# The opening of a convolution and feed-forward kernel: x of units 0 and 1 loaded at once, w_in in two column halves, new orders for the first four tiles

## The chip, the core and the metric

The kernel runs on one core of a Trainium2 chip. Such a core has five engines with an instruction queue each: TensorE (PE), VectorE (DVE), ScalarE (ACT), GpSimd (POOL) and SyncE (SP). Here SP issues most of the transfers, POOL issues those of `w_in`, and 16 DMA engines carry all of them. An engine works its queue strictly in order; between engines only semaphores hold things back. Matmuls write to PSUM, from which DVE and ACT read; POOL works on SBUF alone. The metric is the device time of one execution in microseconds (us); lower is better.

## The reference, cut to what matters

```python
batch, seq, d_model = (8, 4096, 192); kernel_size = 7; n_heads = 8        # x, weight
n_tokens, d_model, d_ff = (32768, 192, 2048)                              # w_in, w_out
w = softmax(weight, axis=-1)                                              # 8 heads x 7 taps
x_pad = np.concatenate([np.zeros((B, 6, D)), x], axis=1)
out = np.einsum('hk,bskhg->bshg', w, x_unf)                               # causal convolution along the sequence
h = out.reshape(B * S, D) @ w_in
g = h * np.cos(h)
return g @ w_out
```

All inputs and the output are fp32; the kernel multiplies in bf16.

## The kernel before

The 32,768 tokens are cut into 32 units of 1,024 tokens, and each unit into two tiles of 512, so there are 64 tiles. A unit goes through these stages:

- **Load** (`load_unit`, L72, and `load_edges`, L68): SP transfers x of a unit, 768 KB, and 96 KB of edge rows (16 tokens at each border between blocks of 128). Two buffers.
- **Cast** (`cast_unit`, L175): POOL turns x into bf16 (`x_bf`, two buffers). Half of unit 0 is cast by ACT, at the start.
- **Convolution** (`conv_part`, L214): matmuls with a banded matrix, in two parts of four heads. A part is two PE steps, `c1` and `c2`; then ACT copies each of its two banks to `ct` (L205; `ec1`, `ec2`). In the first two tiles a part is four matmuls over all 128 rows, in one PE step, and a unit has both its parts in one tile, called `d` and `c`.
- **Doubling and turning**: POOL writes a second copy beside each block (`double_unit`, L245), and an SP transposing transfer (`turn_unit`, L249) makes `cT`, the transposed convolution result. POOL then mends the first columns of each block from the edge rows (`mend_edges`, L257).

A tile `t` then runs eight column pairs `j` through three engines:

- PE step `h<j>` (`mm1`, L339): six matmuls, `w_in` columns against `cT`, into a PSUM buffer `h` of two banks. Three such buffers form a ring, which the convolution of later tiles uses too.
- ACT and DVE step `s<j>` (`gcu`, L351): ACT computes the cosine as a shifted sine (L354), DVE multiplies it with `h` (L358) and writes `g`. The buffer `h` is free when DVE is through.
- PE steps `m<n>` (`mm2_step`, L364): n steps of the second product, `g` against `w_out`, into the banks `o_ps0` and `o_ps1`. A phase is 32 steps and fills one half tile; from the second phase on a step is two matmuls on the two row halves of the array, the second belonging to the phase before. In the first phase it is one. At the end of a phase (`q`, `p` in the orders) ACT copies the bank to SBUF (L389; `Q`, `P`), and SP stores every tile.

The order on PE, ACT and DVE is written out by hand as strings. `PE_ORDER` and `ACT_ORDER` hold for all tiles; `PE_FIRST` and `ACT_FIRST` replace them in the first two (called slots t=0 and t=1 here). DVE follows the order of the `s` steps. A word `h0a` is the half `h0` of the first two blocks. The matmul steps are counted through: whatever the order, the 64 tiles hold the same steps, and a later tile starts with 8 steps of its predecessor's phase done.

Before the tiles the kernel builds the band matrix from the softmax of the weights, convolves the first half of unit 0 (`conv_first`, L286) and turns it on PE (`turn_first`, L305). The word `r` in slot 0 stands for `conv_rest` (L318), the other half of unit 0, followed by its doubling and turning, the load of unit 2, and POOL's cast of `w_out` to bf16 (L445).

SP issues in order: x of unit 0, first half (L87); then, behind a wait for DVE's `summed` (L271), its second half and unit 1; then, behind a wait for a copy of `conv_first` (L301), `w_out` in four transfers (L91); the turning of unit 0's second half; units 2 and 3. POOL issues `w_in` early, in two row halves, all columns at once (L84, L134). It casts unit 0's second half at L281 and unit 1 at L332.

Of the kernel before, what the change touches and what calls it, by code (L numbers as in the profile page):

```python
# [11 lines left out]
ALU = mybir.AluOpType  # L12
# [4 lines left out]
def kernel(  # L17
# [8 lines left out]
    nc = tc.nc  # L26
# [7 lines left out]
    NB = T // 128  # L34
    U = 1024
    NU = NTOK // U
    UB = U // 128
# [3 lines left out]
    NP = NF // 2  # L41
# [26 lines left out]
    def load_edges(u, queue=nc.sync):  # L68
        queue.dma_start(out=x_tiles[u][:, UB, :],
                          in_=xf[u * U - 8 : u * U - 8 + U, :].rearrange("(n t) d -> n t d", t=128)[:, 0:16, :])  # L70

    def load_unit(u, n0=0, n1=UB, queue=nc.sync):  # L72
        if n0 == 0:
            x_tiles[u] = xin.tile([128, UB + 1, D], FP32, name="x_f")
        queue.dma_start(out=x_tiles[u][:, n0:n1, :],
                          in_=xf[u * U + n0 * 128 : u * U + n1 * 128, :].rearrange("(n p) d -> p n d", p=128))
# [3 lines left out]
    w = consts.tile([128, NC, NP, 128], BF16)  # L80
    w_src = moe_w_in.rearrange("(m k) (t f) -> t m k f", k=NC, t=2)
    HP = NP // 2

    def load_w(t):  # L84
        nc.gpsimd.dma_start(out=w[64 * t : 64 * t + 64].rearrange("p k j f -> p k (j f)"), in_=w_src[t])

    load_unit(0, 0, NB)  # L87
    wo_f = consts.tile([128, NP, 2, D], FP32)
    wo_src = moe_w_out.rearrange("(i j p) d -> p j i d", i=2, p=128)

# [40 lines left out]
    nc.vector.memset(band, 0.0)  # L131
    for q, copy in enumerate((nc.vector.tensor_copy, nc.scalar.copy, nc.scalar.copy)):
        copy(out=mask[32 * q + 32 : 32 * q + 64], in_=mask[0:32])
    for t in range(2):  # L134
        load_w(t)
    nc.gpsimd.memset(xb0[:, 0, :], 0.0)
    ident = consts.tile([128, 128], BF16)
    nc.gpsimd.memset(ident, 0.0)
# [18 lines left out]
    sync_dep = mybir.DependencyInfo(mybir.DependencyClass.Sync, mybir.DependencyReason.DATA)  # L157
# [17 lines left out]
    def cast_unit(u, n0=0, n1=UB + 1, copy=nc.gpsimd.tensor_copy):  # L175
        bf[u] = xb0 if u == 0 else xbf_pool.tile([128, UB + 1, D], BF16, name="x_bf")

        o = 1 if u == 0 else 0
        copy(out=bf[u][:, n0 + o : n1 + o, :].rearrange("p n (h k r) -> p (n h) k r", k=NC, r=R),  # L179
             in_=x_tiles[u][:, n0:n1, :].rearrange("p n (h r k) -> p (n h) k r", k=NC, r=R))  # L180
        if u and u % UPS == 0:
            nc.gpsimd.memset(bf[u][0:8, UB, :], 0.0)
        bf.pop(u - 2, None)
# [65 lines left out]
    def turn_unit(u, n0=0, n1=UB + 1):  # L249
        ct = ct_tiles.pop(u)  # L250
        if u not in cT:
            cT[u] = cT_pool.tile([128, UB + 1, NC, 128], BF16, name="cT")
        nc.sync.dma_start_transpose(out=cT[u][:, n0:n1].rearrange("p n c k -> p (n c) k"),
                                    in_=ct[:, n0:n1].rearrange("p n c t k -> p (n c t k)"))
        cT.pop(u - 2, None)
# [9 lines left out]
    prod = consts.tile([128, HQ, E, K], BF16)  # L265
    nc.vector.tensor_tensor(out=prod, in0=mask.rearrange("p (o e) k -> p o e k", o=1).to_broadcast([128, HQ, E, K]),
                            in1=wn.rearrange("p h (o k) -> p h o k", o=1).to_broadcast([128, HQ, E, K]), op=ALU.mult)
    diag = consts.tile([128, HQ, E], FP32)
    summed = nc.vector.tensor_reduce(out=diag, in_=prod, axis=mybir.AxisListType.X, op=ALU.add)

    tc.add_manual_dep(nc.sync.nop().ins, summed.ins.name, sync_dep, reason="order of the transfers")  # L271
    load_unit(0, NB, UB)
    load_unit(1)
    load_edges(1)

    three = {"D": nc.vector.tensor_copy, "A": nc.scalar.copy, "P": nc.gpsimd.tensor_copy}
    for i, k in enumerate("DPDPDPADPDPADPAD"):
        q, rows = divmod(i, 4)
        three[k](out=band[32 * rows : 32 * rows + 32, HQ * q : HQ * (q + 1), 32 * rows : 32 * rows + E],  # L279
                     in_=diag[32 * q : 32 * q + 32])  # L280
    cast_unit(0, NB, UB)  # L281
    ct_tiles[0] = ct_pool.tile([128, UB + 1, NC, 2, 64], BF16, name="ct")
    cT[0] = cT_pool.tile([128, UB + 1, NC, 128], BF16, name="cT")
    copies = [nc.scalar.copy, nc.vector.tensor_copy]

    def conv_first():  # L286

        banks = o_banks()
        for half in range(2):
            for h in range(H):  # L290
                for prev in range(2):
                    nc.tensor.matmul(  # L292
                        out=banks[half][:, 0 : 2 * D].rearrange("p (n k h r) -> p h n k r", n=2, k=NC, h=H)[:, h],
                        lhsT=band[:, h, 128 * prev : 128 * prev + 128],
                        rhs=bf[0][:, 2 * half + 1 - prev : 2 * half + 3 - prev, h * G : (h + 1) * G].rearrange(
                            "p n (k r) -> p n k r", k=NC),
                        start=(h == 0 and prev == 0), stop=(h == H - 1 and prev == 1), skip_group_check=True)
            m = copies[half](out=ct_tiles[0][:, 2 * half : 2 * half + 2].rearrange("p n k t w -> p (n k) t w"),  # L298
                             in_=banks[half][:, 0 : 2 * D].rearrange("p (m t w) -> p m t w", t=1, w=64).to_broadcast(
                                 [128, 2 * NC, 2, 64]))  # L300
        tc.add_manual_dep(nc.sync.nop().ins, m.ins.name, sync_dep, reason="order of the transfers")  # L301
        load_wo(0)
        load_wo(1)
# [25 lines left out]
    conv_first()  # L329
    turn_first(0)  # L330
    turn_first(1)
    cast_unit(1)  # L332

# [55 lines left out]
    def store(t, b0=0, b1=2):  # L391
# [8 lines left out]
    PE_ORDER = "h0 m7 c1 m6 c2 m4 h1 m7 q h2 h3 m12 h4 m10 h5 m10 h6 h7 p m8"  # L400
    ACT_ORDER = "s0 ec1 ec2 s1 Q s2 s3 s4 s5 P s6 s7"

    PE_FIRST = ["h0a h0b h1 r h2 h3 h4 d1 d2 h5 h6 c1 c2 h7 p m12",
                "h0 m8 h1 m12 q h2 h3 h4 m4 d1 d2 m8 h5 m8 h6 c1 c2 m8 h7 m4 p m8"]
    ACT_FIRST = ["s0a s0b s1 s2 s3 s4 ed1 ed2 s5 s6 ec1 ec2 s7", "s0 s1 s2 s3 s4 ed1 ed2 s5 s6 ec1 ec2 P s7"]

    HALVES = {"": (0, NB), "a": (0, NB // 2), "b": (NB // 2, NB)}
    step = 0
    for t in range(NT + 2):
        u, second = divmod(t, TPU)  # L410
        cu, cc = (u + TPU, second) if t >= TPU else (1 + t, 1)
        conv = {"c": conv_part(cu, cc, ring_banks if t else o_banks, t < TPU) if cu < NU else iter(())}
        if t < TPU:
            conv["d"] = conv_part(cu, 0, ring_banks if t else o_banks, True)
        act, done, h = (ACT_ORDER if t > 1 else ACT_FIRST[t]).split(), set(), {}

        def flush():
            while act:
                k = act[0]
                need = {"P": "p", "Q": "q", "e": k[1:2] + "2"}.get(k[0], "h" + k[1:])  # L420
                if need not in done:
                    return
                act.pop(0)
                if k == "P" and 0 <= t - 1 < NT:
                    evac(t - 1, 0)
                elif k == "Q" and 0 <= t - 2 < NT:
                    evac(t - 2, 1)
                elif k[0] == "e":
                    next(conv[k[1]], None)
                elif k[0] == "s" and t < NT:  # L430
                    gcu(t, int(k[1]), h.pop(k[1:]), *HALVES[k[2:]])

        for k in (PE_ORDER if t > 1 else PE_FIRST[t]).split():
            if k[0] == "h" and t < NT:
                h[k[1:]] = mm1(t, int(k[1]), *HALVES[k[2:]])
            elif k[0] in conv:
                next(conv[k[0]], None)
            elif k == "r":
                conv_rest()
                double_unit(0, NB, UB)  # L440
                turn_unit(0, NB, UB)
                load_unit(2)
                load_edges(2)
                for q in range(2):
                    nc.gpsimd.tensor_copy(out=wo[:, q * HP : (q + 1) * HP], in_=wo_f[:, q * HP : (q + 1) * HP])  # L445
            elif k[0] == "m":
                for q in range(step, step + int(k[1:])):
                    mm2_step(q)
                step += int(k[1:])
            elif k[0] == "p":  # L450
                assert step % (2 * STEPS) == 0
            elif k[0] == "q":
                assert step % (2 * STEPS) == STEPS
            done.add(k)
            flush()

            if k == "q":
                if second == 0 and t and u + 1 < NU:
                    turn_unit(u + 1)
                    mend_edges(u + 1)  # L460
                if t == 1:
                    turn_unit(1)
                    cast_unit(3)
                    mend_edges(1)
                if second == 0 and u + 3 < NU:
                    cast_unit(u + 3)
                if second == 1 and t > 1 and cu < NU:
                    double_unit(cu)
                if t == NT + 1:
                    store(NT - 1, 1, 2)  # L470
            if k == "p":
                if t < NT + 1 and 0 <= t - 2:
                    store(t - 2)
                if t == NT:
                    store(NT - 1, 0, 1)
                if second == 1 and u + 4 < NU:
                    load_unit(u + 4)
                    load_edges(u + 4)
        if t == 0:
            double_unit(1)  # L480
            load_unit(3)
            load_edges(3)
            cast_unit(2)
        if t == 1:
            double_unit(2)
# [30 lines left out]
```

## Time and profile before

| what | us |
|---|---|
| median of 8 runs (lowest to highest) | 720.67 (720.34 to 720.84) |
| the profiled execution, by its own time | 720.64 |
| its span, first to last instruction | 718.9 |
| PE busy over the span | 707.2 (98%) |
| ACT busy, DVE busy, POOL busy | 617.7, 611.5, 149.7 |
| slot 0 starts on PE / slot 1 / slot 2 / slot 3 / slot 4 | 10.43 / 22.25 / 35.74 / 46.58 / 57.42 |

The profile page gives each engine's busy time, the chain of work that ended last and the costliest groups of instructions. The timeline lists merged instructions in order: start, duration, engine, source line, operation, output and inputs, count, and in brackets the idle time before it with what ended that. A view of windows gives the busy time of each engine in chosen stretches, the granted PE clock, the share of the 16 DMA engines that was busy, and GB/s. All times count from the start of the span. A slot's start in the table is the first matmul of its `h0`. From slot 2 on the slots are 10.84 us apart.

### The profile page before, as it was taken

Reading aid. Unit: us, or ns where it says so; the run is one execution under the profiler, and the core shown is the slowest. Engines: PE = TensorE matmul, PEld = TensorE weight load, DVE = VectorE, ACT = ScalarE, POOL = GpSimd, SP = SyncE. Lnnn points to the kernel's source line nnn. Section 1 sums busy time; section 2 is a strip of 40 time slices with the busy share of each in tenths; the row PEclk is TensorE's granted clock in tenths of the full one; section 3 lists DMA queues with packets and bytes.
Section 4 is the critical chain, followed back from the end, with each engine's and each line's share of the span. In section 5 each row is a group of like instructions: output and inputs, shape, how many; then the busy total and the mean of one; then the engine's idle time right before and its main releaser. Section 6 shows DMA issues by size and latency. Waiting matters only on the chain.

```text
span 718.9 us, 26316 instructions
## 1 busy us (share of the span) xinstructions
PE 707.2 (98%) x11827; PEld 530.1 (74%) x11827; DVE 611.5 (85%) x536; ACT 617.7 (86%) x781; POOL 149.7 (21%) x124
## 2 busy tenths in 40 slices
PE   7899999999999999999999999999999999999997
PEld 3577777777777777777777777777777777777776
DVE  6788888888888888888888888888888888888984
ACT  7888888888898898888888888888888888888884
POOL 5621122221122221122220222220122221121000
PEclk9999999999999999999999999999999999999999
DMA  8755544455534356534455434566434455324312
GB/s 215 182 123 144 133 94 129 86 139 145 123 108 114 92 144 145 111 108 111 105 145 145 116 103 100 117 144 145 108 110 95 124 145 142 103 68 89 80 46 67
DMA packets 183664, 85.24 MB, mean 119 GB/s; under 512 B 111616, under 2 KB 183168, under 8 KB 183552
## 3 DMA queue, kind: packets, MB, share of 16 engines
q1 hardware_dynamic: 183128, 82.78, 46.9%
q8 instruction: 92, 1.51, 0.9%
q0 software_dynamic: 416, 0.79, 0.8%
q14 instruction: 20, 0.16, 0.1%
q10 hardware_dynamic: 8, 0.00, 0.0%
HBM read 31.36 MB, written 25.17 MB: 79 GB/s over the span
## 4 chain that ended last, share of the span: by engine, by line
PE 95%; DMA 2%; POOL 1%; DVE 1%; ACT 0%; issue 0%; SPq 0%; DVEq 0%; POOLq 0%
PE o_ps L377 46%; PE h L347 45%; PE h L190 3%; DMA wo_f<-in_moe_w_out_dram 1%; DMA x_f<-in_x_dram 1%; PE h L377 0%; POOL x_bf L179 0%; DVE band L279 0%; POOL wo L445 0%; DVE g L358 0%; DVEq L511 0%; ACT cs L354 0%; POOL mask L128 0%; DVE ct L298 0%; ACT o_sb L389 0%
## 5 line engine op out<-in xcount | busy, mean ns | idle before, releaser
L358 DVE TENSOR_TENSOR g<-h,cs 128x1024 bf16<-128x1024 f32 (+1 forms) x513 | 603.6, 1218 | 94.1 <-ACT cs L354 89.2
L354 ACT ACTIVATE cs<-h 128x1024 bf16<-128x1024 f32 (+1 forms) x513 | 511.3, 1026 | 59.3 <-PE h L347 52.2
L377 PEld LDWEIGHTS <-g 64*128 64x128 bf16 x8192 | 362.2, 94 | 86.0 <-SPq L164 1.2
L377 PE MATMUL o_ps<-wo,g 64*128 64x192 bf16 x8128 | 423.8, 243 | 1.7 <-ACT o_sb L389 0.6
L347 PE MATMUL h<-cT,w 64*128 64x512 bf16 (+1 forms) x3078 | 398.4, 376 | 0.3 <-DVE cT L316 0.2
L347 PEld LDWEIGHTS <-w 64*128 64x128 bf16 x3078 | 154.7, 94 | 85.4 <-issue 1.1
L259 POOL COPY cT<-cT 128x144 bf16<-128x144 bf16 x31 | 9.5, 307 | 496.0 <-DMA cT<-ct 359.4
L179 POOL CAST x_bf<-x_f 128x1728 bf16<-128x1728 f32 (+1 forms) x32 | 80.5, 2516 | 9.1 <-DMA x_f<-in_x_dram 8.9
L205 ACT CAST ct<-h 128x432 bf16<-128x432 f32 x120 | 56.4, 522 | 27.5 <-PE h L190 26.9
L389 ACT COPY o_sb<-o_ps 128x384 f32<-128x384 f32 x127 | 60.1, 473 | 4.9 <-PE o_ps L377 4.9
L247 POOL COPY ct<-ct 128x1728 bf16<-128x1728 bf16 (+1 forms) x32 | 51.2, 1602 | 18.8 <-ACT ct L205 18.2
L190 PE MATMUL h<-x_bf,band 64*128 64x216 bf16 (+1 forms) x472 | 42.7, 254 | 1.0 <-POOL x_bf L179 1.0
L190 PEld LDWEIGHTS <-band 64*128 64x128 bf16 (+1 forms) x496 | 22.2, 94 | 7.3 <-issue 4.7
L377 PE MATMUL h<-wo,g 64*128 64x192 bf16 x64 | 5.8, 243 | 0.0
L105 PE MATMUL o_ps<-zero 128*128 128x512 bf16 x12 | 4.3, 510 | 1.3 <-DVE zero L100 1.3
L190 PE MATMUL o_ps<-x_bf,band 128*128 128x96 bf16 (+1 forms) x24 | 1.9, 222 | 2.6 <-POOL x_bf L179 2.6
L105 PEld LDWEIGHTS <-zero 128*128 128x128 bf16 x15 | 1.5, 115 | 2.9 <-DVE zero L100 1.3
L205 ACT CAST ct<-o_ps 128x432 bf16<-128x432 f32 (+1 forms) x6 | 2.4, 461 | 1.2 <-PE o_ps L190 1.2
L445 POOL CAST wo<-wo_f 128x1536 bf16<-128x1536 f32 x2 | 2.9, 1470 | 0.8 <-DMA wo_f<-in_moe_w_out_dram 0.8
L292 PE MATMUL o_ps<-x_bf,band 128*128 128x48 bf16 x32 | 1.5, 183 | 1.2 <-ACT x_bf L179 0.8
L292 PEld LDWEIGHTS <-band 128*128 128x128 bf16 x32 | 1.2, 96 | 1.9 <-POOL band L279 1.9
L389 ACT COPY o_sb<-h 128x384 f32<-128x384 f32 x1 | 0.5, 478 | 2.4 <-PE h L377 2.4
(47 smaller groups left out, 27.7 us busy)
## 6 DMA issues: line engine op xcount, KB each, us to landing
out_dram<-o_sb SPq DMA_DIRECT2D x63, 384.0 KB
x_f<-in_x_dram SPq DMA_DIRECT2D x31, 768.0 KB
x_f<-in_x_dram SPq DMA_DIRECT2D x31, 96.0 KB
wo_f<-in_moe_w_out_dram SPq DMA_DIRECT2D x4, 384.0 KB
x_f<-in_x_dram SPq DMA_DIRECT2D x2, 384.0 KB
w<-in_moe_w_in_dram POOLq DMA_DIRECT2D x2, 384.0 KB, 6.3
cT<-ct SPq DMA_TRANSPOSE x32
out_dram<-o_sb SPq DMA_DIRECT2D x2, 192.0 KB
```

Source lines behind the costliest of these rows:

```text
L105: nc.tensor.matmul(out=bank, lhsT=zero[:, 0:128], rhs=zero, start=True, stop=True)
L179: copy(out=bf[u][:, n0 + o : n1 + o, :].rearrange("p n (h k r) -> p (n h) k r", k=NC, r=R), in_=x_tiles[u][:, n0:n1, :].rearrange("p n (h ...
L190: return nc.tensor.matmul(out=ps[i // 2][:, 0 : (n1 - n0) * 2 * G].rearrange("p (n k i r) -> p i n k r", n=n1 - n0, k=NC, i=2)[:, i % 2], ...
L205: copy(o[:, :, 0, :], i[:, :, 0, :])
L247: nc.gpsimd.tensor_copy(out=ct[:, n0:n1, :, 1, :], in_=ct[:, n0:n1, :, 0, :])
L259: nc.gpsimd.tensor_copy(out=cT[u][:, 0:UB, :, 0 : K - 1], in_=cT[u][:, UB].rearrange("p c (n t) -> p n c t", t=16)[:, :, :, 8 : 8 + K - 1])
L347: nc.tensor.matmul(out=h[:, i, n0 * 128 : n1 * 128], lhsT=w[rows, k, j, :], rhs=c[rows, m0 + n0 : m0 + n1, k, :], start=(k == 0), stop=(k ...
L354: nc.scalar.activation(out=cs[:, :, part], in_=h[:, :, part], func=AF.Sin, bias=math.pi / 2.0, scale=1.0)
L358: nc.vector.tensor_tensor(out=g_tiles[t][:, 2 * j : 2 * j + 2, part], in0=h[:, :, part], in1=cs[:, :, part], op=ALU.mult)
L377: m = nc.tensor.matmul(out=o_ps[tt, b][:, si * D : (si + 1) * D], lhsT=g_tiles[tt][rows, f, s * 128 : (s + 1) * 128], rhs=wo[rows, f // 2, ...
L389: nc.scalar.copy(o_sb[t][:, 2 * b : 2 * b + 2, :].rearrange("p s d -> p (s d)"), o_ps.pop((t, b))[:, 0 : 2 * D])
L445: nc.gpsimd.tensor_copy(out=wo[:, q * HP : (q + 1) * HP], in_=wo_f[:, q * HP : (q + 1) * HP])
```

## The change

- SP issues x of unit 0 whole and unit 1 with its edges at the very start, without the wait for `summed`.
- `w_in` is loaded in two column halves, each in two row-half transfers. The first half (columns of `h0` to `h3`) is issued where all of it was; the second (`h4` to `h7`) on POOL behind the cast of unit 0's second half. The cast of unit 1 follows it on POOL, ahead of the work of the tiles.
- In the block `r`, the load of unit 2 is issued on SP ahead of the turning of unit 0's second half instead of behind it.
- `PE_FIRST` and `ACT_FIRST` now cover four slots. Slot 0 holds no second-product steps; `r` comes between `h0a` and `h0b`; the two convolution parts of unit 1 come after `h2` and `h5`. Slot 1 begins with 14 second-product steps. The slots 2 and 3 begin with second-product steps and their convolution, before `h0`. At the start of slot 4 the count of steps is as before.

```diff
-    def load_w(t):
-        nc.gpsimd.dma_start(out=w[64 * t : 64 * t + 64].rearrange("p k j f -> p k (j f)"), in_=w_src[t])
+    def load_w(j0, j1):
+        for t in range(2):
+            nc.gpsimd.dma_start(out=w[64 * t : 64 * t + 64, :, j0:j1, :].rearrange("p k j f -> p k (j f)"),
+                                in_=w_src[t, :, :, j0 * 128 : j1 * 128])
 
     load_unit(0, 0, NB)
+    load_unit(0, NB, UB)
+    load_unit(1)
+    load_edges(1)
...
-    for t in range(2):
-        load_w(t)
+    load_w(0, HP)
...
-    summed = nc.vector.tensor_reduce(out=diag, in_=prod, axis=mybir.AxisListType.X, op=ALU.add)
-
-    tc.add_manual_dep(nc.sync.nop().ins, summed.ins.name, sync_dep, reason="order of the transfers")
-    load_unit(0, NB, UB)
-    load_unit(1)
-    load_edges(1)
+    nc.vector.tensor_reduce(out=diag, in_=prod, axis=mybir.AxisListType.X, op=ALU.add)
...
     cast_unit(0, NB, UB)
+    load_w(HP, NP)
+    cast_unit(1)
...
     turn_first(1)
-    cast_unit(1)
...
-    PE_FIRST = ["h0a h0b h1 r h2 h3 h4 d1 d2 h5 h6 c1 c2 h7 p m12",
-                "h0 m8 h1 m12 q h2 h3 h4 m4 d1 d2 m8 h5 m8 h6 c1 c2 m8 h7 m4 p m8"]
-    ACT_FIRST = ["s0a s0b s1 s2 s3 s4 ed1 ed2 s5 s6 ec1 ec2 s7", "s0 s1 s2 s3 s4 ed1 ed2 s5 s6 ec1 ec2 P s7"]
+    PE_FIRST = ["h0a r h0b h1 h2 d1 d2 h3 h4 h5 c1 c2 h6 h7 p",
+                "m14 h0 m4 h1 m8 h2 m6 q h3 m6 h4 m10 d1 d2 m7 h5 m8 c1 c2 m1 p h6 m2 h7",
+                "m10 c1 m6 c2 m1 h0 m13 q h1 h2 m10 h3 m7 h4 m5 h5 m10 p h6 h7",
+                "m7 c1 m5 c2 m5 h0 m8 h1 m7 q h2 h3 m15 h4 m4 h5 m13 h6 h7 p m8"]
+    ACT_FIRST = ["s0a s0b s1 s2 s3 ed1 s4 ed2 s5 ec1 ec2 s6 s7", "s0 s1 s2 s3 s4 ed1 ed2 s5 ec1 P s6 ec2 s7",
+                 "ec1 ec2 s0 Q s1 s2 s3 s4 s5 P s6 s7", "ec1 ec2 s0 s1 Q s2 s3 s4 s5 P s6 s7"]
...
                 conv_rest()
                 double_unit(0, NB, UB)
-                turn_unit(0, NB, UB)
                 load_unit(2)
                 load_edges(2)
+                turn_unit(0, NB, UB)
```

More of the change, by code (lines that the diff above doesn't have):

```diff
@@ L414 @@
             conv["d"] = conv_part(cu, 0, ring_banks if t else o_banks, True)
-        act, done, h = (ACT_ORDER if t > 1 else ACT_FIRST[t]).split(), set(), {}
+        act, done, h = (ACT_ORDER if t >= len(ACT_FIRST) else ACT_FIRST[t]).split(), set(), {}
         def flush():
@@ L431, in flush @@
                     gcu(t, int(k[1]), h.pop(k[1:]), *HALVES[k[2:]])
-        for k in (PE_ORDER if t > 1 else PE_FIRST[t]).split():
+        for k in (PE_ORDER if t >= len(PE_FIRST) else PE_FIRST[t]).split():
             if k[0] == "h" and t < NT:
```

## The prediction

> **What bounds the kernel now.** I read the page first (its chain of work), then the timeline of the first 60 us, then windows cut at the slots' starts, then windows for the transfers.
>
> ```profile
> PE 95%; DMA 2%; POOL 1%; DVE 1%; ACT 0%; issue 0%; SPq 0%; DVEq 0%; POOLq 0%
> ```
>
> The chain is PE's for 95%, so the run ends when PE has worked off a fixed list of matmuls. An edit to the opening pays by the time at which PE enters slot 4, from where both kernels hold the same work. The windows of slots 0 to 2 (length, busy PE, PEld, DVE, ACT, POOL; granted clock, DMA share, GB/s):
>
> ```profile
> 10.43:22.25 11.82, 8.68 (x89) 4.83 (x91) 9.20 (x11) 9.81 (x16) 7.66 (x6) 1.00 0.98 263
> 22.25:35.74 13.49, 11.78 (x160) 8.10 (x159) 9.72 (x9) 10.30 (x14) 8.13 (x5) 1.00 0.76 191
> 35.74:46.58 10.84, 10.84 (x191) 8.40 (x187) 8.43 (x8) 8.93 (x13) 0.18 (x1) 1.00 0.79 190
> ```
>
> Slot 2 has no idle PE; slots 0 and 1 have 3.14 and 1.71 us of it, while the DMA engines are full in slot 0 (share 0.98). The timeline says who is late:
>
> ```profile
> 2.96 1.40 POOL L85 DMA_DIRECT2D w<-in_moe_w_in_dram  x2
> 11.86 1.22 POOL L179 CAST x_bf<-x_f 128x768 bf16<-128x768 f32 x1 [4.03 <-DMA x_f<-in_x_dram]
> 13.13 0.84 PE L190 MATMUL o_ps<-x_bf,band 128*128 128x96 bf16 x16 [0.97 <-POOL x_bf L179]
> 15.05 2.52 POOL L179 CAST x_bf<-x_f 128x1728 bf16<-128x1728 f32 x1 [1.97 <-DMA x_f<-in_x_dram]
> 17.62 0.53 PE L190 MATMUL o_ps<-x_bf,band 128*128 128x216 bf16 x4 [1.60 <-POOL x_bf L179]
> 18.36 1.57 SPq L253 DMA_TRANSPOSE cT<-ct  x1
> 22.25 0.39 PE L347 MATMUL h<-cT,w 64*128 64x512 bf16 x1
> 29.02 0.53 PE L190 MATMUL h<-x_bf,band 128*128 128x216 bf16 x4 [1.02 <-POOL x_bf L179]
> 35.09 0.84 PE L377 MATMUL o_ps<-wo,g 64*128 64x192 bf16 x16 [0.59 <-ACT o_sb L389]
> ```
>
> Three times a load of x is late, so its cast, so the convolution on PE, and all behind it in PE's queue. The transfers by windows (same columns):
>
> ```profile
> 3.60:4.40 0.80, 0.80 (x3) 0.30 (x2) 0.33 (x3) 0.76 (x3) 0.80 (x3) 1.00 0.06 17
> 4.40:9.40 5.00, 3.73 (x45) 1.98 (x44) 3.88 (x12) 3.88 (x7) 2.36 (x9) 1.00 1.03 145
> 10.20:18.40 8.20, 5.45 (x61) 3.14 (x62) 6.27 (x10) 6.20 (x10) 4.57 (x4) 1.00 1.10 322
> 19.60:21.60 2.00, 1.43 (x13) 0.65 (x12) 1.60 (x2) 2.00 (x5) 1.24 (x2) 1.00 1.04 198
> ```
>
> Full from 4.4 to 18.4: w_in first (to about 10.2, 5.8 us), then x and w_out at 322 GB/s; from 19.6 the turning of unit 0 (2.0 us). Slot 1's `h0` starts at 22.25, 0.65 after the turning's last bytes.
>
> **Unit prices**, from slots 2 and 3: an `h` step 0.65 us of PE (41.67 to 42.32), a second-product step 0.083 (10 in 42.32 to 43.15), a convolution part 0.36 to 0.38; PE start of `h` to ACT 0.87, ACT to DVE 1.05, one multiply to the next 1.14, DVE start to a free ring buffer 1.3.
>
> **Removed: the waits for x.** Unit 0's second half no longer waits for `summed` (over at 5.98), nor its bytes for w_in. x is 1.28 MB behind the first half's last byte at 3.6: 4.0 us at 322 GB/s, 7.6 alone, 10.5 if it shares with the first half of w_in (2.9 us, half of 5.8). POOL is free of its band copies at 7.8; cast 1.2 to 9.05, w_in issue 1.40 to 10.45, unit 1's cast 2.5 to 13.0, against 17.57 before. PE: `h0a` is held by the turned blocks (10.3) and w_in, whose first half lands by about 11.0 (10.5 plus a landing of some 0.5) against 10.68 (a weight load of `h0a` waited for it until then): at most 0.5 later, which slot 1's wait below hides. Then `r` at about 11.5 (13.13 before), unit 1's first part after `h2` at 13.9 with x_bf ready: the waits of 0.97 and 1.60 are gone.
>
> Next is DVE: `s1` at 14.5, then 1.14 each, and 0.9 for ACT's `ec1 ec2` ahead of `s6`: `s7` 21.9 (22.68 before), `h7` on PE 19.2 to 19.85, slot 1's `m14` (14 x 0.083) to 21.0.
>
> **Added: a wait for the turning.** Slot 1's `h0` needs unit 0's second half turned, and that transfer now stands in SP's queue behind unit 2 (0.885 MB), which is behind w_out (1.57 MB); w_in's second half, issued at 9.05, starts 1.44 later (2.96 to 4.4 before), 10.5, and shares the engines. From 10.5: w_in 2.9 + w_out 4.9 + unit 2 2.75 + turning 2.0 = 23.05, and 0.65 to its use: 23.7. On SP it is issued after w_out (13.3 in the timeline) and unit 2's two issues (0.92 + 0.66 there), 14.9; the doubling it needs is done on POOL near 13.8. Both hide under the queue of bytes. POOL's two casts of w_out (1.47 each) follow by about 20, ahead of the second-product steps that need them. One of the 16 engines ran behind before (POOL's cast of w_out at 20.51 waited for it, although the DMA share was 0.18 from 18.4 to 19.6); it could add up to 1.0. I take 24.0. Lower end 22.0: x, w_out and unit 2 at the 367 GB/s of the best stretch near 10.5 to 11.5, w_in's half 2.4, turning 1.8, use 0.5. Upper end 25.0: the lagging engine and halves of w_in at 3.2. So PE idles from 21.0 to 24.0 with all of slot 1 queued behind `h0`, its second-product steps too; ACT and DVE run dry after `s7` (21.9 + 1.2 = 23.1). The gain of slot 0 is spent there.
>
> **Slots 1 to 3 from that `h0` on.** After: 24 `h` 15.6 + 186 steps (14 to 200) 15.4 + convolution 1.5 = 32.5, and stalls that I find by walking the new orders with the prices above: `m2` behind `P`'s copy 0.5, `h7` for a ring buffer 0.2, 0.2 in slots 2 and 3: 33.4. Before: 15.6 + 188 steps 15.6 + 1.5 = 32.7, but 57.42 - 22.25 = 35.17, so 2.5 of stalls (1.02 and 0.59 in the rows above, the rest for ring buffers). The early load of unit 2 (landed by 22, cast by 25, wanted at 30) and the new orders take 1.6 away, two steps done ahead 0.2. The turning of unit 1, issued at `q` (27.5), needs 6 to 8 (25.63 to the mend at 33.62; 61.42 to 67.48): 35.5 at most, used at 36.7.
>
> **Sum.** Slot 4 at 24.0 + 33.4 = 57.4 against 57.42: removed 1.8, added 24.0 - 22.25 = 1.75, net 0.0. The profiled execution took 720.64, 0.03 under the median; I give 720.6. With 22.0 to 25.0: -2.0 to +1.0, its own range 718.6 to 721.6. About 0.2%, 1.44 us, is what a measurement of this kernel tells from no change.
>
> **A rule against the change.** Longest wait in the rows above: 1.60, clock 1.00 in every window; the new wait is near 3. The Trainium skill ("TensorE: Matmul & The Clock Gate", Part 1, what's actually happening) says that after an idle window of about 3.4 us the PE clock halves until it has been busy as long. No row here has such a gap. By the page the sum would be up to 1.7 us more (an estimate, half of 3.4), 722.3; by the rows 720.6.
>
> **Rivals.**
> - *The turning isn't late*: the queue moves it ahead or w_in's halves hide beside x. Then `h0` follows `m14` at 21.0 to 22.0: slot 4 at 54.4 to 55.4, 717.6 to 718.6. For: 367 GB/s was reached. Against: a full share with nothing left to hide in.
> - *w_in's second half is late* (the slower side). `h4` to `h7` and all behind wait for it; wanted at 15.8. Each microsecond past 18.7 moves slot 4 by one, since `m14` ends 5.3 after `h4`: 18.7 + 5.3 = 24.0. If it comes after w_out (10.5 + 4.9 + 2.9 + 0.5 = 18.8): +0.1. If after unit 2 as well (21.5): +2.8, 723.4. For: it's the later issue beside a full SP queue. Against: before, it was x, issued from 6.0 on, that stood back until w_in was through, near 9.4 to 10.2. The Trainium skill ("DMA: Bandwidth & Descriptors", Queues, rings and completion order) has the engines take turns between queues; that row does not show turns, and with turns this half would land near 16.8, costing nothing.
> - *Halved rows of w_in cost per row, not per byte*: 5.8 a half, so the turning is used 2 x 2.9 later, or 2.9 where it hides: +2.9, 723.5. For: 145 GB/s at the start. Against: 276 GB/s from 9.4 to 10.2.
>
> **How the numbers follow.** Turning lands 22.6 to 25.4 (no change beyond 0.2%): 0.45. Not late: 0.25. w_in late 0.12, w_in per row 0.10, the turning past 25.4 for another reason 0.08: 0.30 slower. The range takes the turning at 21.8 below (718.4) and most of the two slower rivals above, to 723.0.
>
> **What would show it.** Right: PE idle some 3 us before slot 1's first `h`, released by DMA cT; unit 1's cast over by 13 to 14; no wait for POOL ahead of the convolutions of slots 0 and 1; slot 4 near 57.4, and 10.84 a slot from there. Wrong: `h0` of slot 1 within 0.5 of `m14`; a wait for DMA w ahead of `h4`; a granted clock under 1.00; or stalls in slots 1 to 3 that my walk does not have.

## The result and the profile after

The median went from 720.53 us (32 executions, 720.20 to 720.99) to **723.13 us** (11 executions, 721.63 to 727.13): a ratio of 1.0037, 95% interval 1.0029 to 1.0046. The kernel became slower by 2.6 us, 0.13 above the upper end of the forecast range. It also became uneven: its executions spread over 5.5 us where those of before spread over 0.8. The profiled execution took 724.66 by its own time (span 722.9), which is 4.02 above the profiled one of before and 1.5 above the median of after.

The chain of waits is still PE's; one point of the shares has gone from POOL to PE:

```profile
PE 96%; DMA 2%; DVE 1%; ACT 0%; POOL 0%; issue 0%; DVEq 0%; SPq 0%; POOLq 0%
```

Slot 4 starts at 61.38 instead of 57.42. These 3.96 us are nearly the whole difference of 4.02, so all that matters happens before slot 4. PE's timeline of slot 0 and of the start of slot 1 (start, duration, engine, line, operation, count, idle time before it):

```profile
11.45 0.50 PE L348 MATMUL h<-cT,w 64*128 64x256 bf16 x5 [0.75 <-DMA w<-in_moe_w_in_dram]
11.88 0.85 PE L194 MATMUL o_ps<-x_bf,band 128*128 128x96 bf16 x16
14.54 0.53 PE L194 MATMUL o_ps<-x_bf,band 128*128 128x216 bf16 x4
...
17.43 1.47 PE L348 MATMUL h<-cT,w 64*128 64x512 bf16 x11 [0.87 <-DMA w<-in_moe_w_in_dram]
...
21.36 1.32 PE L378 MATMUL o_ps<-wo,g 64*128 64x192 bf16 x14
24.69 0.61 PE L348 MATMUL h<-cT,w 64*128 64x512 bf16 x4 [2.02 <-DMA cT<-ct]
```

The waits for POOL's casts ahead of the convolutions are gone (no bracket at 11.88 and 14.54). In their place stand two waits for `w_in` (0.75 and 0.87) and one of 2.02 for the turning, with all of slot 1 behind it. SP's timeline and the last links of the chain before slot 1 tell why the turning is late:

```profile
9.72 2.57 SPq L98 DMA_DIRECT2D wo_f<-in_moe_w_out_dram  x4
12.47 1.64 SPq L75 DMA_DIRECT2D x_f<-in_x_dram  x1
14.16 3.26 SPq L69 DMA_DIRECT2D x_f<-in_x_dram  x1
17.53 4.70 SPq L257 DMA_TRANSPOSE cT<-ct  x1
```

```profile
10.13 7.40 DMA wo_f<-in_moe_w_out_dram
17.53 7.11 DMA cT<-ct
24.64 0.05 issue
24.69 0.82 PE h L348 x6
```

Unit 2's two issues take SP from 12.47 to 17.42. The turning is issued at 17.53 and lands at 24.64. So far this is the path that was forecast, used 0.7 later than the 24.0 taken. What follows slot 1's first matmuls is not. Windows from the end of slot 0 on (length; busy time and count of PE, PEld, DVE, ACT, POOL; granted clock, DMA share, GB/s):

```profile
22.68:24.69 2.01, 0.00 (x0) 0.00 (x1) 2.01 (x2) 0.65 (x1) 2.01 (x2) 1.00 0.91 204
24.69:25.96 1.27, 1.27 (x15) 0.79 (x16) 0.11 (x1) 0.41 (x1) 1.27 (x1) 1.00 1.06 351
25.96:32.78 6.82, 6.82 (x46) 4.45 (x44) 3.67 (x3) 3.69 (x4) 2.85 (x2) 0.50 0.55 65
32.78:37.22 4.44, 4.44 (x72) 3.23 (x70) 2.52 (x3) 2.99 (x4) 0.12 (x1) 1.00 0.76 170
37.22:61.38 24.16, 24.01 (x399) 18.06 (x399) 20.14 (x18) 21.55 (x29) 6.51 (x6) 1.00 0.41 102
```

From 25.96 to 32.78 the granted clock is 0.50. PE is busy all the time and gets through 46 matmuls in 6.82 us, where 72 took 4.44 us just behind it. No wait is named, because PE waits for nothing: it is slow. From slot 1 to slot 4 PE needs 36.69 us; the forecast had 33.4, before it was 35.17.

This execution is slower than most of its kernel. The mean granted clock of an execution tells how much of it ran at half clock: a mean of 0.996 or 0.997 leaves room for one stretch of 3.41 us in the opening, 0.995 for two as here, 0.998 for one or none, 0.999 and above for none. (An estimate: 3.41 us at half speed take 0.0024 off the mean of some 722 us, and up to 2.5 us at the very end of the span, the most that the profiled executions show there, take off up to 0.0017 more.) Of the eleven executions seven have 0.996 or 0.997 and take 721.63 to 724.27; the one with 1.0 takes 721.83. So the clock is a part of the spread and not all of it.

### The profile page after: what moved, and what is told of

It reads as the page before. It is cut to its first block, busy times and chain, and to the rows that moved or that the text cites. A ratio compares the mean times of both kernels' runs of the same rounds, so it can differ in the third digit from the quotient of the medians.

```text
span 722.9 us, 26322 instructions
## 1 busy us (share of the span) xinstructions
PE 711.6 (98%) x11827; PEld 532.1 (74%) x11827; DVE 611.7 (85%) x536; ACT 617.9 (85%) x781; POOL 150.8 (21%) x126
## 3 DMA queue, kind: packets, MB, share of 16 engines
q8 instruction: 92, 1.51, 0.8%
## 4 chain that ended last, share of the span: by engine, by line
PE 96%; DMA 2%; DVE 1%; ACT 0%; POOL 0%; issue 0%; DVEq 0%; SPq 0%; POOLq 0%
PE o_ps L378 47%; PE h L348 45%; PE h L194 3%; DMA wo_f<-in_moe_w_out_dram 1%; DMA cT<-ct 1%; PE h L378 0%; DVE band L278 0%; DVE g L359 0%; DVEq L515 0%; ACT cs L355 0%; ACT o_sb L390 0%; POOL mask L133 0%; DVE ct L299 0%; ACT mask L138 0%; DVE diag L273 0%
## 5 line engine op out<-in xcount | busy, mean ns | idle before, releaser
L86 POOL DMA_DIRECT2D w<-in_moe_w_in_dram x4 | 2.7, 668 | 0.0
```

## The experiments

Two theories were set against each other. **Theory A**: the order on SP makes the turning late, PE stands idle ahead of slot 1, and the idle time halves the clock behind it; the clock is the term that the forecast left out. **Rival R2**: the second half of `w_in` comes late, and slot 0 and the transfers behind it slip. **Rival R1**: the new orders of slots 1 to 3 stall PE by themselves. Both rivals hold the order on SP to be harmless; that was tried on the kernel before as well. The runs carry the labels under which their expectations are on record; e4 and e9 change the kernel before, all others the changed one.

All runs side by side. "Half clock" is what the profiled execution shows outside the last microseconds; "slot 1" and "1 to 4" are PE's start of slot 1 and its time from there to slot 4 in that execution.

| kernel | median (lowest to highest) | ratio to before [95%] | slot 1 | 1 to 4 | half clock |
|---|---|---|---|---|---|
| before | 720.53 (720.20–720.99) | | 22.25 | 35.17 | none |
| after | 723.13 (721.63–727.13) | 1.0037 [1.0029, 1.0046] | 24.69 | 36.69 | 6.83 us from 25.96 |
| e1 after, turning ahead of unit 2 | 720.53 (719.35–721.47) | 0.9998 [0.9990, 1.0007] | 22.67 | 33.80 | none |
| e2 after, zero matmuls in the gap | 722.40 (721.57–723.32) | 1.0022 [1.0013, 1.0031] | 26.11 | 33.34 | 3.41 us from 18.75 |
| e3 after, all of w_in at once | 722.57 (719.47–723.37) | 1.0023 [1.0015, 1.0032] | 25.81 | 33.80 | 6.83 us from 12.38 |
| e4 before, unit 2 ahead of turning | 725.22 (723.31–726.64) | 1.0064 [1.0051, 1.0077] | 23.77 | 36.22 | 3.41 us from 24.12 |
| e9 as e4, zero matmuls in the gap | 722.16 (721.88–722.85) | 1.0022 [1.0014, 1.0031] | 24.35 | 34.56 | none |
| e11 after, second half of w_in early | 720.88 (719.37–722.27) | 1.0001 [0.9992, 1.0010] | 23.59 | 35.01 | 3.41 us from 23.98 |
| e12 as e11, zero matmuls in the gap | 720.14 (719.24–722.39) | 0.9998 [0.9989, 1.0007] | 23.66 | 33.33 | none |
| e14 as e12, eight instead of five | 720.51 (719.64–721.14) | 0.9999 [0.9990, 1.0008] | 23.47 | 33.34 | none |
| e7 after, turning ahead of half of w_out | 720.64 (719.46–724.12) | 1.0004 [0.9994, 1.0014] | 22.68 | 35.41 | none |
| e8 as e7, and as e11 | 719.40 (718.44–720.45) | 0.9985 [0.9976, 0.9994] | 21.07 | 35.06 | none |
| e10 as e8, two steps moved | 719.35 (718.16–720.78) | 0.9985 [0.9976, 0.9993] | 20.84 | 34.05 | none |

### e1: the turning put back ahead of unit 2

```diff
                 double_unit(0, NB, UB)
+                turn_unit(0, NB, UB)
                 load_unit(2)
                 load_edges(2)
-                turn_unit(0, NB, UB)
```

> The changed kernel with one thing undone: SP issues the turning of unit 0's second half ahead of unit 2's load again. Theory A (the turning behind unit 2 makes slot 1 late, and the thin PE work around that wait halves the clock): w_out lands near 20.8 as in the changed kernel, the turning 1.2 to 2 later, so slot 1's h0 follows m14 (ending at 22.7) almost without a wait, clock 1.00 throughout; slot 4 starts at 22.8 + 33.4 = 56.2, so about 719.4. Rival R1 (the new orders of slots 1 to 3 stall PE by themselves) and R2 (the late second half of w_in is what costs): the time stays at or above 721.3.

Measured: 720.53, the time of before. One moved line takes back all 2.6 us. The profiled execution (719.69) has the turning issued at 14.70 and slot 1 at 22.67, right behind its 14 steps, with no bracket; the clock stays at 1.00:

```profile
14.70 5.06 SPq L257 DMA_TRANSPOSE cT<-ct  x1
```

```profile
22.67:56.47 33.80, 33.57 (x527) 25.15 (x527) 28.21 (x25) 29.68 (x39) 13.21 (x9) 1.00 0.62 144
```

From slot 1 to slot 4 it takes 33.80, near the walked 33.4. So the new orders do what the walk said when the clock lets them, and R1 is out. `h4` still waits 1.40 us for `w_in` here, so that wait alone doesn't make the loss. What isn't explained: the median lies 0.8 above the profiled execution, although nine of its eleven executions show a mean clock of 0.999 to 1.0.

### e2: the gap filled, the transfers left alone

```diff
-                "m14 h0 m4 h1 m8 h2 m6 q h3 m6 h4 m10 d1 d2 m7 h5 m8 c1 c2 m1 p h6 m2 h7",
+                "m14 w9 h0 m4 h1 m8 h2 m6 q h3 m6 h4 m10 d1 d2 m7 h5 m8 c1 c2 m1 p h6 m2 h7",
...
+            elif k[0] == "w":
+                keep_warm(int(k[1:]), o_pools[1].tile([128, T], FP32, name="o_ps1"))
```

> The changed kernel with nine matmuls of zeros (128x512, about 0.22 us each, 2 us in all) on PE between m14 and h0 of slot 1, into a bank that is free; transfers untouched. Theory A: the turning still lands near 24.6 and h0 starts at 24.7, but PE is busy meanwhile and the clock stays at 1.00; slot 4 starts at 24.7 + 33.4 = 58.1, about 721.3, and the executions lie within 0.5 of each other instead of 5. R1: no effect, 723.1 with the same spread.

Measured: 722.40, 0.7 under the changed kernel where 1.8 was expected, and a spread of 1.75 instead of 5.5. The profiled execution shows why this run settles less than was hoped: its clock fell earlier, inside slot 0, where PE had waited 0.50 and 1.74 us shortly before. Behind the filled gap it stayed at 1.00:

```profile
18.75:22.17 3.42, 3.07 (x15) 1.14 (x16) 2.45 (x2) 3.18 (x6) 1.47 (x1) 0.50 1.64 299
22.17:26.11 3.94, 3.63 (x26) 1.97 (x24) 2.36 (x2) 1.55 (x2) 3.57 (x3) 1.00 0.78 138
26.11:59.45 33.34, 33.19 (x523) 24.60 (x524) 26.00 (x23) 28.58 (x37) 11.12 (x8) 1.00 0.54 120
```

Slot 1 to slot 4 took 33.34 instead of 36.69: the 3.3 us between the walk and the changed kernel are the clock's. But the loss is not tied to the gap ahead of `h0` alone; slot 0 is thin enough for it as well. The ten executions part by their mean clock: five with 0.999 or 1.0 take 721.57 to 722.31, five with 0.994 to 0.997 take 722.50 to 723.32.

### e3: w_in whole instead of in column halves

```diff
-    load_w(0, HP)
+    load_w(0, NP)
...
-    load_w(HP, NP)
```

> The changed kernel with w_in loaded at the first place with all columns, in two row halves, as before. Theory A: h4 no longer waits for w_in, so m14 ends near 21.2, but the bytes ahead of the turning are the same and it lands at 24.2 to 24.7; the wait grows to 3 us, the clock still halves: 722 to 725. R2 (w_in's late half is the cost): at least the 1.2 us that h4 waited comes back, and with it the clock: 720 to 721.5.

Measured: 722.57, inside theory A's range, but not by its path: slot 1's `h0` follows its 14 steps without a wait for the turning. The late second half is gone, but now PE waits for the whole of `w_in` at the start of slot 0 (1.23 and 1.91 us, landing 11.45 and 13.63), and the clock is 0.50 from 12.38 on:

```profile
12.38:19.20 6.82, 5.52 (x40) 2.80 (x41) 2.09 (x5) 2.76 (x5) 3.98 (x4) 0.50 1.11 307
25.81:59.61 33.80, 33.57 (x528) 25.17 (x528) 28.22 (x25) 29.68 (x39) 12.54 (x9) 1.00 0.47 99
```

So the halves are not the fault by themselves: a `w_in` loaded at once behind x costs as much, by another wait and the same drop.

### e4 and e9: the one line in the kernel before, and the price of the clock

e4 takes the kernel before and moves only the turning behind unit 2. e9 adds eight zero matmuls ahead of its slot 1.

```diff
                 double_unit(0, NB, UB)
-                turn_unit(0, NB, UB)
                 load_unit(2)
                 load_edges(2)
+                turn_unit(0, NB, UB)
```

```diff
-                "h0 m8 h1 m12 q h2 h3 h4 m4 d1 d2 m8 h5 m8 h6 c1 c2 m8 h7 m4 p m8"]
+                "w8 h0 m8 h1 m12 q h2 h3 h4 m4 d1 d2 m8 h5 m8 h6 c1 c2 m8 h7 m4 p m8"]
```

> The kernel before with one thing of the change: unit 2's load issued on SP ahead of the turning of unit 0's second half. Theory A: the turning lands near 22.2 + 2.9 = 25.1, slot 1 starts at 25.2 in place of 22.25, the wait of 1.02 for unit 2's cast goes: +1.9 with the clock at 1.00, 722.5; up to 3.4 more where the clock halves. R1 and R2: the queue order isn't the cause, so within 0.7 of 720.5.

> The kernel before with unit 2's load ahead of the turning (725.2 in its own run), and eight matmuls of zeros (1.75 us) on PE ahead of slot 1's h0, where PE waits 1.5 for the turning. Theory A: the wait itself costs 1.5 to 2 and the halved clock the rest, so with PE kept busy 722 to 722.7, spread under 1.5. Rival (the lateness is all of it, the clock costs nothing): 725.2 as without them.

Measured: 725.22 and 722.16. In the profiled execution of e4 PE waited 1.47 us, less than the 1.60 that the kernel before has in slot 0, and 0.35 us after it had begun again the clock halved:

```profile
23.77 1.15 PE L347 MATMUL h<-cT,w 64*128 64x512 bf16 x6 [1.47 <-DMA cT<-ct]
```

```profile
24.12:27.54 3.42, 3.42 (x22) 2.05 (x17) 1.23 (x1) 1.05 (x2) 2.02 (x2) 0.50 0.56 181
```

e9 stands in the same place with the gap filled (the `zero` matmuls end just before `h0`), and six `h` matmuls take 0.82 instead of 1.15:

```profile
22.42 1.90 PE L105 MATMUL o_ps<-zero 128*128 128x512 bf16 x7
24.35 0.82 PE L347 MATMUL h<-cT,w 64*128 64x512 bf16 x6
```

```profile
24.35:27.80 3.45, 3.45 (x39) 2.52 (x41) 1.45 (x2) 2.05 (x2) 2.18 (x2) 1.00 0.62 193
```

The transfers are the same and the work is eight matmuls more, yet it is faster by 3.06 us (725.22 - 722.16). That is the clock's price, measured; what is left over before, 722.16 - 720.53 = 1.6, is the price of the late turning as such, with what the zero matmuls may cost. In the two profiled executions, where e4 has one stretch at half clock, slot 1 to slot 4 differ by 36.22 - 34.56 = 1.66. The other executions of e4 had more of it: 723.31 goes with a mean clock of 0.997, 724.36 and 724.48 with 0.995, 725.97 to 726.64 with 0.992, by the estimate above one, two and three stretches. This also refutes the view that the order on SP is harmless: alone, in the kernel before, it costs 4.7 us.

### e11 and e12: the second half of w_in issued 1.3 us earlier

e11 moves one line of the changed kernel; e12 also puts five zero matmuls (`w5`, as in e2) between `m14` and `h0` of slot 1.

```diff
-    cast_unit(0, NB, UB)
     load_w(HP, NP)
+    cast_unit(0, NB, UB)
     cast_unit(1)
```

> The changed kernel with w_in's second half issued on POOL ahead of the cast of unit 0's second half, and nothing else. Theory A: h4 hardly waits and m14 ends near 21.2, but the turning still stands behind unit 2 and lands at 24 to 24.6; PE waits 3 instead of 2, so the clock halves at least as often: 722 to 724. R2 (the late half of w_in is the cost of the change): it goes below 721.

> The changed kernel with the second half of w_in issued early, as in e11, and five zero matmuls into a free PSUM bank between m14 and h0 of slot 1 (they add nothing to the output). Transfers are those of e11; only PE's idle stretch of 1.72 us ahead of h0 shrinks to about 0.3 us. Theory A (the clock drop behind that gap is what separates the executions of e11 near 719.6 from those at 720.9 to 722.3): the upper group vanishes, median 719.4 to 720.3, granted clock 1.00 behind 20 us. Rival (the groups come from when the transfers land, the clock follows or is beside it): both groups stay, median near 720.9 as in e11, with the turning landing at different times.

Measured: 720.88 for e11. Theory A's number for it was wrong and R2's was right: the late half of `w_in` is a real part of the loss, worth 2.25 us at the median (723.13 - 720.88; the size is rough, since this median is the lowest time of the slower of two groups, below). Its issue at 7.79 instead of 9.06 lets it land at 13.89 instead of 17.39, `h4` no longer waits for it, and the turning lands at 23.55 instead of 24.64. The windows of the transfers of the changed kernel and then of e11 show the reason:

```profile
8.50:10.00 1.50, 1.45 (x22) 0.78 (x19) 1.23 (x2) 1.07 (x2) 1.50 (x3) 1.00 0.86 143
10.00:12.50 2.50, 1.57 (x26) 1.00 (x24) 0.84 (x2) 1.03 (x3) 0.89 (x2) 1.00 0.80 86
```

```profile
8.50:10.00 1.50, 1.45 (x22) 0.79 (x19) 1.22 (x2) 1.07 (x2) 1.46 (x2) 1.00 1.28 180
10.00:12.50 2.50, 1.26 (x18) 0.68 (x16) 0.85 (x2) 0.71 (x3) 1.69 (x2) 1.00 1.02 149
```

By 12.5 e11 has moved 1.5 x 180 + 2.5 x 149 = 643 KB since 8.5, the changed kernel 1.5 x 143 + 2.5 x 86 = 430 KB. Everything behind it on the queues, the turning last of all, comes earlier.

But e11 falls in two groups: five executions at 719.37 to 719.83 with a mean clock of 0.999 to 1.0, and six at 720.88 to 722.27 with 0.996 to 0.998. e12 asks what parts them. Its median is 720.14, inside theory A's band, with nine of eleven at or below 720.65 (two remain, 721.31 and 722.39, at 0.997 and 0.998). The two profiled executions stand in the same place, slot 1 at 23.59 and 23.66; the stretch behind it, e11 first:

```profile
23.98:27.39 3.41, 3.41 (x23) 2.09 (x20) 1.23 (x1) 1.74 (x2) 1.54 (x2) 0.50 0.58 194
```

```profile
24.05:27.46 3.41, 3.41 (x39) 2.36 (x37) 1.89 (x2) 2.66 (x3) 1.33 (x2) 1.00 0.57 191
```

In the same 3.41 us with the same transfers, PE issues 23 matmuls at half clock and 39 at full clock. From slot 1 to slot 4 that makes 35.01 against 33.33, so one such stretch costs 1.68 us. In e12 PE still waits 1.51 us behind the zero matmuls, and the clock holds; one of 1.72 in e11 and one of 1.47 in e4 were enough for the drop. So the length of that wait alone doesn't decide.

### The condition of the drop, and e14

The clock's stretches in the opening of these traces are all multiples of one length: 3.41, 6.83 (2), 13.65 (4), 17.07 (5), 20.48 (6). So the clock changes on a grid of 3.41 us, and the grid's place differs: the first stretch at full clock begins between 4.64 and 7.41. I cut every trace along its own grid and looked at PE's busy time in each window. The window before the drop in the changed kernel and in e11:

```profile
22.55:25.96 3.41, 1.39 (x17) 0.79 (x16) 2.25 (x2) 1.19 (x2) 3.41 (x2) 1.00 0.97 254
```

```profile
20.57:23.98 3.41, 1.69 (x20) 1.29 (x19) 2.81 (x3) 1.88 (x3) 3.41 (x3) 1.00 0.85 167
```

The emptiest windows that no drop followed, in e7 and in the kernel before:

```profile
10.77:14.18 3.41, 1.73 (x29) 1.32 (x31) 0.67 (x2) 1.00 (x3) 2.40 (x1) 1.00 0.94 164
```

```profile
14.88:18.30 3.42, 1.82 (x18) 0.78 (x14) 2.61 (x4) 3.04 (x4) 3.25 (x3) 1.00 1.09 325
```

| behind the window the clock | PE busy in the 3.41 us |
|---|---|
| halves | 1.39 (after), 1.45 (e3), 1.51 (e4), 1.65 (e2), 1.69 (e11) |
| stays at 1.00 | 1.73 (e7), 1.82 (before), 1.90 (e12), all others of the opening more |

The border lies between 1.69 and 1.73: half of 3.41 is 1.71. A window in which PE is idle for half of the time is enough. (The ends of matmuls are modelled in the traces, so the border is no sharper than that.) This also gives a reason why executions of one kernel differ: an idle stretch of 1.72 counts in full only if it lies inside one grid window, which 3.41 - 1.72 = 1.7 us of 3.41 possible places allow, about half (an estimate). Six of eleven executions of e11 were in the upper group.

e14 tries the reading: e12 with eight zero matmuls in place of five (`w8`), so that no window comes near the border.

> As e12, with eight zero matmuls instead of five between m14 and h0 of slot 1 (they add nothing to the output). A reading of the traces so far: the granted clock changes only on a grid of 3.41 us whose place differs from execution to execution, and it halves behind a grid window in which PE was idle for 1.72 us or more (five windows), never behind one of 1.69 or less. If so, eight zero matmuls (about 1.9 us) leave at most 0.9 us of the stretch of 2.7, no window reaches 1.7, and the upper group goes altogether: all executions within 719.2 to 721.0, median 719.6 to 720.4 (h0 may be held up to 0.3 us by the zero matmuls), clock 1.00 behind slot 0. If the drop has another condition, one or two in ten stay above 721.2 as in e12.

Measured: the eleven executions lie between 719.64 and 721.14, where e11 went up to 722.27 and e12 to 722.39, and none has a mean clock under 0.998. That supports the reading but doesn't prove it: 721.13 and 721.14 lie just above the 721.0 expected, and three executions have 0.998, which doesn't rule out one stretch (e11's profiled execution has one and 0.998). The median, 720.51, is 0.1 above the band that was expected, so the zero matmuls may cost more than the 0.3 allowed for them; what else lifts it wasn't found. The wait that is left:

```profile
21.02 1.90 PE L110 MATMUL o_ps<-zero 128*128 128x512 bf16 x8
23.47 0.82 PE L348 MATMUL h<-cT,w 64*128 64x512 bf16 x6 [0.55 <-DMA cT<-ct]
```

### e7, e8 and e10: the turning still earlier

e7 issues the second half of `w_out` behind the turning instead of ahead of it. e8 adds e11's line. e10 also moves two second-product steps of slot 1 from before `h1` to behind it.

```diff
         load_wo(0)
-        load_wo(1)
...
+                turn_unit(0, NB, UB)
+                load_wo(1)
                 load_unit(2)
                 load_edges(2)
-                turn_unit(0, NB, UB)
```

```diff
-                "m14 h0 m4 h1 m8 h2 m6 q h3 m6 h4 m10 d1 d2 m7 h5 m8 c1 c2 m1 p h6 m2 h7",
+                "m14 h0 m2 h1 m10 h2 m6 q h3 m6 h4 m10 d1 d2 m7 h5 m8 c1 c2 m1 p h6 m2 h7",
```

> The changed kernel with the turning of unit 0's second half issued on SP ahead of unit 2's load and of the second half of w_out. Theory A: the turning lands by 18 to 19, and w_in's second half shares the engines with half of w_out only, so it lands near 16 and h4 hardly waits; m14 ends near 21.4 and slot 1's h0 follows at once; slot 4 at 21.4 + 33.4 = 54.8, about 718.0, the clock at 1.00. If instead something else in slot 0 holds it (DVE, ring buffers, the first half of w_in), no better than the variant with the turning ahead of unit 2 alone, 719.5 to 720.5.

> As the variant with the turning ahead of w_out's second half, and w_in's second half issued on POOL ahead of the cast of unit 0's second half instead of behind it (7.9 in place of 9.06). Theory A: the w_in half lands a microsecond earlier, h4 does not wait at all; DVE then sets slot 0 and m14 ends at 21.0 as in the walk of the prediction: 717.5 to 718. If the bytes merely change places with w_in's first half and x, no gain over that variant.

> The faster variant (turning ahead of w_out's second half, w_in's second half early), with slot 1's start as m14 h0 m2 h1 m10 instead of m14 h0 m4 h1 m8: the step that needs the second half of w_out, which cost PE 1.33 of waiting, comes after h1. ACT and DVE then have h1 to work on during the wait: 0.5 to 1.0 less than that variant's 719.4, so 718.4 to 718.9; if the wait is only moved, 719.4.

Measured: 720.64, 719.40 and 719.35. e7 missed by 2.6: slot 1 starts at 22.68, but the wait moves on to the next transfer, `w_out`, whose cast POOL can now start only at 24.06. e8's row shows the same wait, shorter:

```profile
23.61 0.24 PE L377 MATMUL o_ps<-wo,g 64*128 64x192 bf16 x1 [1.33 <-POOL wo L449]
```

e8 starts slot 1 at 21.07, right behind its 14 steps, and beats the kernel before by 0.15% (0.9985, 0.9976 to 0.9994), 1.2 us, though not by the 2.5 to 3 expected. e10 takes the wait away in its profiled execution (slot 1 to slot 4 in 34.05, 718.16 by its own time, the fastest of its eleven), but its median is that of e8. So the change does hold a gain once the turning isn't behind unit 2 and `w_in`'s second half isn't late.

## Why the prediction was wrong

**The clock is the step that failed.** The forecast was 720.6, no change; 723.13 is 2.5 more. The paragraph "A rule against the change" named the mechanism, and the sum left it at nothing: "by the rows 720.6". The profiled execution had 6.83 us at half clock, and 36.69 against the walk's 33.4 makes 3.3 us of it. e4 and e9 price the drop at 3.06 by their medians; for one stretch e4 and e9 give 1.66, e11 and e12 1.68. The page of the Trainium skill that the prediction cites ("TensorE: Matmul & The Clock Gate", Part 1, what's actually happening) has the clock halve after an idle window of about 3.4 us. The estimate from it, half of 3.4 or 1.7, fits one stretch of 3.41 us; the changed kernel's profiled execution had two of them in a row, and windows of this length are in these traces too. But the forecast took an idle window as one without any work, and that is where it went wrong: a window counts as idle here when PE is busy for less than about half of it, and no single wait ahead of a drop was longer than 2.02 us. Two of the prediction's own signs of being wrong came, the clock under 1.00 and a wait for `w_in` at `h4`. The row "Longest wait in the rows above: 1.60, clock 1.00 in every window" was no comfort: the kernel before had a window with 1.82 us of work in 3.42, 0.1 us from the border. A new wait of 3 us, as forecast, must fill more than half of a grid window in most places that the grid can take; the term should have stood in the sum at one or two times 1.7, which is 722.3 to 724.0.

**The late turning** was right. SP's order and the bytes ahead of it came out as worked: 24.69 against the 24.0 taken, inside the bounds of 22.0 to 25.0. PE's wait was 2.02 and not 3, since `h4`'s wait let `m14` end at 22.68 and not at 21.0. The 0.7 us missing goes with `w_in`'s second half: from 10.0 to 12.5 all transfers together moved 86 GB/s, where the sum had that half alone at some 136 (0.39 MB in 2.9 us). With it earlier, in e11, the turning was used at 23.59. Its issue, forecast for 14.9, came at 17.53, since the issues of unit 2 held SP for 4.9 us instead of the 1.6 of before. e9 prices the lateness at 1.6 in the kernel before.

**The removed waits** were right: POOL's second-half cast at 7.89, no wait for POOL ahead of the convolutions, and unit 1's cast done by 14.48, later than the 13 to 14 forecast but soon enough. The gain is seen in e1's profiled execution, which has everything but the order on SP and enters slot 4 at 56.47 instead of 57.42; e1's median, 720.53, doesn't show it.

**The walk through slots 1 to 3**, 33.4, was right wherever the clock stayed up: 33.80 in e1, 33.34 in e2, 33.33 in e12.

**The sum**: slot 4 at 24.0 + 33.4 = 57.4 was forecast. In the profiled execution it was 24.69 + 33.4 + 3.3 = 61.4: 0.7 from the turning, 3.3 from the clock. The median execution, 723.13, has a mean clock of 0.997 and so one stretch: 720.6 + 0.7 + 1.7 = 723.0 (an estimate, if its turning came as late). That 723.13 lies so near the upper end of the range, 723.0, is chance: that end was drawn from the two slower rivals, and neither came as described.

**The rivals.** "The turning isn't late" did not happen, and its price was too good: e8, where that is so, took 719.40 against the 717.6 to 718.6 worked out. "w_in's second half is late" was half right: it landed at 17.39, short of the 18.7 from which it should have cost anything, and still cost some 2.25 us. In e11, with that half earlier, the turning came 1.1 earlier and five of eleven executions kept the clock (`h4`'s wait as such was over in time: the `m14` behind it ended 2.0 ahead of the turning). Neither picture of the queues was right throughout: from 10.0 to 12.5 the second half moved 0.18 MB and `w_out`, issued from 9.72 on, 0.04 MB; then it landed among the transfers of `w_out`, at 17.39, 0.6 later than the 16.8 that turns would have given. "Halved rows cost per row" did not happen, as the transfers of the two kernels show: `w_in` is 416 packets before and 832 after, of half the size, and all of them took 88 and 97 us of the 16 engines' time (67.7% of the engines in 2.9 to 11.0, 40.2% in 2.9 to 18.0). A cost per row would have doubled it.

**What stays open**: why the clock came back after one window in e4 and e11 but after two in the changed kernel, although PE was busy throughout the first of them; why e1's executions at full clock lie up to a microsecond above its profiled one, and why the changed kernel's with one stretch lie up to 2.6 us apart; and why the packets of `w_in`'s second half were slow from 10.0 to 12.5.

## What to carry to other kernels

When a change puts a wait into a stretch where PE is already thin, add up PE's idle time over some 3.4 us and, if it nears half, price the clock as well: here a wait of 2.0 us brought matmuls behind it that cost 3.3 us more, and no line of the waits names them; the granted clock and the count of matmuls per window do. A small transfer that an engine queues behind should be issued ahead of large ones that nobody wants yet; one line on SP was worth 2.6 us in the changed kernel and 4.7 in the one before. When the spread between executions grows, here from 0.8 to 5.5 us, a single profile shows only one of several courses: the mean clock of every execution told which of them had the drop.

## What the runs showed of the hardware that was not expected

- The granted clock halves behind a grid window of 3.41 us in which PE was busy for 1.69 us or less, and holds behind 1.73 or more. In the traces it stays at 0.50 for one window or two, and mean clocks of 0.992 in three executions of e4 speak for three; one cost 1.66 and 1.68 us.
- Zero matmuls that nobody needs, put into such a gap, made a kernel faster by 3.06 us (e9 against e4) with the transfers unchanged.
- The issue of one and the same transfer can hold SP for very different times. The turning took 4.70 us in the changed kernel and 5.06 in e1, where the DMA share in that time was 1.25 and 1.33, but 1.57 before and 1.55 in e8, where it was 0.32 and 0.17. The edges of unit 2 took 3.26 in the changed kernel and 0.66 before. That outstanding transfers are the cause is not shown.
